# Weight tiles placed 128 bytes further on in SBUF, in a causal convolution with two gated layers

## The chip, the cores and the metric

One core of one Trainium2 chip. The metric is the device time of the whole program in microseconds (us), the median of several runs.

## The reference, cut to what matters

```python
out = np.einsum('hk,bskhg->bshg', softmax(weight), x_unf)   # causal convolution of 7 taps, 8 heads
x = out.reshape(8192, 192)
h = x @ w_in;  x = (h * sigmoid(h)) @ w_out                 # layer 0: 192 -> 2048 -> 192, SiLU
h = x @ w_in2; x = elu(h) @ w_out2                          # layer 1: the same shape, ELU
```

All of it is asked for in float32 precision; the weights are given as float64 and reach the chip as 64-bit words.

## The kernel before, in words

Tokens lie along the free dimension, 512 at a time: 16 blocks `b`. The 192 features are three groups of 64 rows, and the 2048 hidden features are eight chunks `q` of 256. A **unit** is one (layer, block, chunk): 2 x 16 x 8 = 256 units, run one after the other by the loop at the end of the kernel function.

TensorE works in two row halves of 64 partitions, so that two matmuls of 64 rows run side by side. Such a pair is called a **step** here. For precision each operand is split into a rounded part (hi) and a remainder (lo), both of type float32r. A unit has 19 steps:

- `in_products` (L310): 9 steps that make `h` out of the weights `wi` and the tokens `x_hl`.
- `out_products` (L357), two units later: 10 steps that add to the sums `c` and `ab` out of the weights `wo` and the activations `g_hi`, `g_lo`. In order: 2 steps c from g_hi, 2 steps c from g_lo, 4 steps ab from g_hi, 2 steps ab from g_lo.

Each step loads its weights anew (LDWEIGHTS, PEld in the profile), 128 columns per half, except c from g_lo, which loads 66 columns:

```python
C_LO = HP + 2                                   # 66
order = [("c", w_c, 0), ("c", slice(P, P + C_LO), 1), ("ab", w_hi, 0), ("ab", w_lo, 0), ("ab", w_hi, 1)]
```

The weights live in nine places of two tiles each, `wi` and `wo` (pool `wts`), 3072 bytes per partition each. Every slice that a load reads begins a whole number of 128-column blocks, that is of 512 bytes, after the start of its tile. Since 3072 is six times 512, all loads of the program begin at the same offset modulo 512. The weights come from DRAM into `raw` tiles (`load_w`, L88 and L92), are decoded to float32 in `val` with the help of `mag` (`decode_steps`, L110 to L120), and are split into `wi` and `wo` (`split_w`, L127, L128, L141, L143). All but the first two chunks of layer 0 are decoded while matmuls run.

ScalarE and VectorE turn `h` into `g_hi` and `g_lo` (L326 to L338); SyncE issues every DMA.

SBUF is given out pool by pool, in the order in which the pools are opened: `const`, `wts`, `raw`, `mag_p`, `dec`, and then the tiles of tokens and activations. Per partition, the built program before has these start addresses modulo 512: `wi`, `wo`, `raw`, `mag` and `val` 416, the two `x_raw` tiles 416 and 480, `x_hl`, `g_hi`, `g_lo` and the sums on their way out 32.

Of the kernel before, what the change touches and what calls it, by code (L numbers as in the profile page):

```python
# [9 lines left out]
F32 = mybir.dt.float32  # L10
# [12 lines left out]
P = 128  # L23
# [6 lines left out]
W_IN = 3 * P  # L30
W_OUT = 2 * D
RAW = 3

PLACES = NQ + 1
C_LO = HP + 2


@with_exitstack
def kernel(
# [19 lines left out]
    const = ctx.enter_context(tc.tile_pool(name="const", bufs=1))  # L59
    wts = ctx.enter_context(tc.tile_pool(name="wts", bufs=1))  # L60
    raw = ctx.enter_context(tc.tile_pool(name="raw", bufs=RAW))
    mag_p = ctx.enter_context(tc.tile_pool(name="mag_p", bufs=1))
# [19 lines left out]
    IN, OUT, BOTH = slice(0, W_IN), slice(W_IN, W_IN + W_OUT), slice(0, W_IN + W_OUT)  # L82
# [11 lines left out]
    def words(layer, q, cols):  # L94
        w = raw_t[layer, q].bitcast(I32).rearrange("p (n two) -> p n two", two=2)
        return w[:, cols, 0], w[:, cols, 1]

    def decode_steps(layer, q, cols, val=None, mag=None):


        if (layer, q) not in dec_t:
            if mag is None:
                mag = mag_p.tile([P, W_IN + W_OUT], F32, tag="mag", name="mag")
            if val is None:
                val = dec.tile([P, W_IN + W_OUT], I32, tag="val", name="val")
            dec_t[layer, q] = mag, val
        mag, val = (t[:, cols] for t in dec_t[layer, q])
        lower, upper = words(layer, q, cols)
        return [
            lambda: nc.scalar.activation(  # L110
                out=mag, in_=upper.bitcast(F32), func=ACTF.Abs, scale=2.0**-112
            ),
            lambda: nc.vector.tensor_scalar(
                out=val, in0=lower, scalar1=29, scalar2=None, op0=ALU.logical_shift_right
            ),
            lambda: nc.vector.scalar_tensor_tensor(  # L116
                out=val, in0=upper, scalar=-(2**31), in1=val,
                op0=ALU.bitwise_and, op1=ALU.bitwise_or,
            ),
            lambda: nc.vector.scalar_tensor_tensor(  # L120
                out=val, in0=mag.bitcast(I32), scalar=3, in1=val,
                op0=ALU.logical_shift_left, op1=ALU.bitwise_or,
            ),
        ]
# [5 lines left out]
    def split_w(layer, q, cols, eng):  # L130
        if (layer, q) not in wt:
            wt[layer, q] = [
                wts.tile([P, 2, n], F32R, tag=f"{t}{(layer * NQ + q) % PLACES}", name=t)
                for t, n in (("wi", W_IN), ("wo", W_OUT))
# [13 lines left out]
    tap_raw = const.tile([P, 2, TAPS], F32, name="tap_raw")  # L148
    tap_e = const.tile([P, 2, TAPS], F32, name="tap_e")
    tap_w = const.tile([P, 2, TAPS], F32, name="tap_w")  # L150
    tap_m = const.tile([P, 2], F32, name="tap_m")
    tap_s = const.tile([P, 2], F32, name="tap_s")
    tap_r = const.tile([P, 2], F32, name="tap_r")

# [185 lines left out]
    def out_products(u, part=slice(0, None)):  # L340
# [6 lines left out]
        w_hi, w_c, w_lo = (slice(k * P, (k + 1) * P) for k in range(3))  # L347
        order = [("c", w_c, 0), ("c", slice(P, P + C_LO), 1), ("ab", w_hi, 0), ("ab", w_lo, 0), ("ab", w_hi, 1)]
        order = [(*o, i) for o in order for i in range(2)]
# [73 lines left out]
    def next_w(layer, q, *others, val=None):  # L423
        run(decode_steps(layer, q, BOTH, val), *others)
        if q + RAW < NQ:
            load_w(layer, q + RAW)
# [7 lines left out]
    def first_step(q):  # L434
        steps_w[q] = decode_steps(0, q, BOTH)
        return steps_w[q][1]
# [36 lines left out]
    base = where[0, NB - 1, 0]  # L473
    spare = PLACES - NQ
    for q in range(NQ):
# [11 lines left out]
    with tc.manual_schedule():  # L487
# [7 lines left out]
        ab = conv_steps(0, 0, lambda: ps_h.tile([P, 2, TB], F32, tag="h", name="conv")[:, 0, :])  # L495
        c, c_1 = conv_pool_steps(0, 1), conv_pool_steps(1, 1)
        d_in, d_out = (decode_steps(0, 0, cols) for cols in (IN, OUT))
        run(ab, c)
        run(c_1[:4])
# [122 lines left out]
```

## Time and profile before

| what | value |
|---|---|
| median of 3 runs | 1165.93 us (1165.91 to 1166.46) |
| the profiled execution: its own time | 1166.09 us |
| its span, first to last instruction | 1164.3 us |
| granted TensorE clock, mean | 0.997 |
| PE busy | 1140.6 us, 98% of the span |
| PEld busy | 894.1 us, 77% |
| DVE, ACT, POOL busy | 70%, 55%, 5% |

PE is the matmuls, PEld the weight loads, which run beside them. The chain of waits is followed back from the last instruction; 97% of it lies on PE.

### The profile page before, as it was taken

The numbers are of one execution on the slowest core, as the hardware profiler recorded it, in microseconds if no ns is written. First come the engines' busy times: TensorE is split into PE (matmuls) and PEld (weight loads), VectorE is DVE, ScalarE is ACT, GpSimd is POOL, SyncE is SP. The second block draws the span as 40 slices with busy tenths as digits, with TensorE's granted clock in tenths as the row PEclk, the third lists the DMA queues.
The fourth block names the chain that finished last, engine by engine and source line by source line (L and its number), as shares of the span: only waits on it lengthen the run. The fifth ranks groups of instructions, "written<-read, shape, count | busy, mean of one in ns | idle before, by whom it ended". The sixth has DMA issues, their size and how long they took to land.

```text
span 1164.3 us, 22489 instructions
## 1 busy us (share of the span) xinstructions
PE 1140.6 (98%) x9748; PEld 894.1 (77%) x9748; DVE 819.9 (70%) x957; ACT 643.5 (55%) x761; POOL 57.6 (5%) x67
## 2 busy tenths in 40 slices
PE   4899999999999999999999999999999999999998
PEld 3777777777777777777777777777777777777776
DVE  8965546556555555567767787877878777887876
ACT  7655455555545555456775455555455554555554
POOL 7500000000000000000320000000000000000000
PEclk8999999999999999999999999999999999999999
DMA  6310111110111110143201111101111101111100
GB/s 190 103 49 8 35 42 42 42 37 6 42 42 42 42 24 18 42 136 82 83 8 30 33 42 42 42 15 37 33 42 42 42 15 28 42 42 42 29 23 19
DMA packets 31188, 51.11 MB, mean 44 GB/s; under 512 B 3952, under 2 KB 13936, under 8 KB 31088
## 3 DMA queue, kind: packets, MB, share of 16 engines
q1 hardware_dynamic: 31088, 49.67, 16.5%
q8 instruction: 76, 1.25, 0.4%
q14 instruction: 24, 0.20, 0.1%
HBM read 18.98 MB, written 6.29 MB: 22 GB/s over the span
## 4 chain that ended last, share of the span: by engine, by line
PE 97%; DVE 1%; POOL 1%; ACT 0%; SPq 0%; DMA 0%; issue 0%; DVEq 0%; POOLq 0%
PE h L310 46%; PE ab L357 31%; PE c L357 20%; DMA raw<-in_w_dram 0%; POOL conv L289 0%; PE warm L522 0%; DVE g_lo L338 0%; POOL wi L128 0%; SPq L188 0%; DVE x_hl L128 0%; ACT x_hl L127 0%; SPq L88 0%; POOL x_hl L241 0%; DVE val L116 0%; ACT wi L127 0%
## 5 line engine op out<-in xcount | busy, mean ns | idle before, releaser
L310 PE MATMUL h<-x_hl,wi 64*128 64x512 f32 x4608 | 582.9, 394 | 19.5 <-ACT wi L127 13.7
L310 PEld LDWEIGHTS h<-x_hl,wi 64*128 64x128 f32 x4608 | 435.1, 185 | 127.8 <-ACT wi L127 14.6
L357 PE MATMUL ab<-g_hi,wo 64*128 64x512 f32 x2048 | 279.3, 390 | 0.0
L338 DVE TENSOR_TENSOR g_lo<-h,g_hi 128x1024 fp32r<-128x1024 f32 x128 | 156.5, 1223 | 174.3 <-ACT h L327 174.1
L326 ACT ACTIVATE g_hi<-h 128x1024 fp32r<-128x1024 f32 x128 | 131.2, 1025 | 240.1 <-PE h L310 240.1
L331 ACT ACTIVATE g<-h 128x1024 f32<-128x1024 f32 x128 | 131.6, 1028 | 235.5 <-PE h L310 212.0
L357 PEld LDWEIGHTS ab<-g_hi,wo 64*128 64x128 f32 x2048 | 192.5, 184 | 56.5
L333 DVE SCALAR_TENSOR_TENSOR g<-g,h 128x1024 f32<-128x1024 f32 x128 | 156.0, 1219 | 86.4 <-ACT g L332 85.9
L357 PE MATMUL ab<-g_lo,wo 64*128 64x512 f32 x1024 | 162.1, 394 | 0.0
L338 DVE TENSOR_TENSOR g_lo<-g,g_hi 128x1024 fp32r<-128x1024 f32 x128 | 156.9, 1226 | 4.5
L357 PE MATMUL c<-g_lo,wo 64*66 64x512 f32 (+1 forms) x1024 | 160.0, 390 | 0.0
L357 PE MATMUL c<-g_hi,wo 64*128 64x512 f32 x1024 | 160.0, 390 | 0.0
L332 ACT ACTIVATE g<-g 128x1024 f32<-128x1024 f32 x128 | 135.7, 1060 | 3.5
L327 ACT ACTIVATE h<-h 128x1024 f32<-128x1024 f32 x128 | 130.8, 1022 | 0.0
L357 PEld LDWEIGHTS c<-g_hi,wo 64*128 64x128 f32 x1024 | 96.2, 184 | 22.6
L357 PEld LDWEIGHTS ab<-g_lo,wo 64*128 64x128 f32 x1024 | 96.2, 184 | 22.3
L269 DVE SCALAR_TENSOR_TENSOR conv<-x_raw,tap_w,conv 128x512 f32<-128x512 f32 (+1 forms) x180 | 105.8, 626 | 0.5
L357 PEld LDWEIGHTS c<-g_lo,wo 64*66 64x66 f32 (+1 forms) x1024 | 71.5, 136 | 35.6
L336 DVE CAST g_hi<-g 128x1024 fp32r<-128x1024 f32 x128 | 88.9, 694 | 4.5
L379 DVE TENSOR_TENSOR both<-c,both 128x512 f32<-128x512 f32 x32 | 22.1, 692 | 52.0 <-ACT both L378 52.0
L128 POOL TENSOR_TENSOR wi<-val,wi 128x384 fp32r<-128x384 f32 x11 | 11.6, 1056 | 530.6 <-ACT wi L127 530.6
L128 DVE TENSOR_TENSOR x_hl<-conv,x_hl 64x256 fp32r<-64x256 f32 (+1 forms) x47 | 24.0, 534 | 1.2 <-ACT x_hl L127 0.7
(61 smaller groups left out, 325.6 us busy)
## 6 DMA issues: line engine op xcount, KB each, us to landing
x_hl<-x_hl SPq DMA_DIRECT2D x76, 256.0 KB, 3.9
raw<-in_w_dram SPq DMA_DIRECT2D x16, 512.0 KB, 4.4
x_hl<-x_hl SPq DMA_DIRECT2D x34, 128.0 KB, 3.7
x_raw<-in_xT_dram SPq DMA_DIRECT2D x16, 259.0 KB, 3.8
raw<-in_w_dram SPq DMA_DIRECT2D x32, 128.0 KB, 3.1
out_dram<-o SPq DMA_DIRECT2D x16, 256.0 KB, 2.0
x_raw<-in_xT_dram SPq DMA_DIRECT2D x32, 65.5 KB, 3.0
out_dram<-other SPq DMA_DIRECT2D x16, 128.0 KB, 2.3
```

Of the source, the lines that this page charges most:

```text
L128: eng.tensor_sub(out=lo, in0=src, in1=hi.bitcast(F32))
L269: nc.vector.scalar_tensor_tensor(out=y, in0=x, scalar=w, in1=y, op0=ALU.mult, op1=ALU.add)
L310: nc.tensor.matmul(out=h[:, r, :], lhsT=w[ROWS[r], w_lo, ts(of, P)], rhs=x[ROWS[r], 3 * x_lo + part, :], start=n == 0, stop=n == len(order ...
L326: lambda: nc.scalar.activation(out=hi, in_=h, func=ACTF.Silu),
L327: lambda: nc.scalar.activation(out=g, in_=h, func=ACTF.Silu),
L331: lambda: nc.scalar.activation(out=g, in_=h, func=ACTF.Relu, scale=-1.0),
L332: lambda: nc.scalar.activation(out=g, in_=g, func=ACTF.Exp, scale=-1.0),
L333: lambda: nc.vector.scalar_tensor_tensor(out=g, in0=g, scalar=-1.0, in1=h, op0=ALU.add, op1=ALU.max),
L336: lambda: nc.vector.tensor_copy(out=hi, in_=g),
L338: return steps + [lambda: nc.vector.tensor_sub(out=lo, in0=g, in1=hi.bitcast(F32))]
L357: nc.tensor.matmul(out=acc_t[layer, b, f"{name}{r}"][0:m, :], lhsT=wo[ROWS[r], i, cols], rhs=hi_lo[part][ROWS[r], i, :], start=q == 0 and ...
L379: nc.vector.tensor_add(out=to[:, cols], in0=halves[1][:, cols], in1=to[:, cols])
```

## The change

Two tiles that nothing else uses get unused bytes at their end. `tap_m`, in the first pool, becomes 128 bytes longer, so that all that is placed behind it starts 128 bytes later: `tap_s`, `tap_r`, all `wi` and `wo`, all `raw`, and `mag`. `mag` becomes 384 bytes longer, so that all that is placed behind it starts 128 + 384 = 512 bytes later and keeps its offset modulo 512. In the built program `wi`, `wo`, `raw` and `mag` go from 416 to 32 modulo 512; `val`, `x_raw`, `x_hl`, `g_hi`, `g_lo` and the rest stay where they were modulo 512. Every engine has the same instructions, in the same order and with the same waits; line numbers grow by one or two.

```diff
+LINE = 128
...
-                mag = mag_p.tile([P, W_IN + W_OUT], F32, tag="mag", name="mag")
+                mag = mag_p.tile([P, W_IN + W_OUT + 3 * LINE // 4], F32, tag="mag", name="mag")
+                mag = mag[:, BOTH]
...
-    tap_m = const.tile([P, 2], F32, name="tap_m")
+    tap_m = const.tile([P, 2 + LINE // 4], F32, name="tap_m")[:, 0:2]
```

## Rows read from the trace of the kernel before

**Rows 1.** The page, part 1: busy time, share of the span, instructions.
```profile
PE 1140.6 (98%) x9748; PEld 894.1 (77%) x9748; DVE 819.9 (70%) x957; ACT 643.5 (55%) x761; POOL 57.6 (5%) x67
```
**Rows 2.** The page, part 4: the chain that ended last, by engine.
```profile
PE 97%; DVE 1%; POOL 1%; ACT 0%; SPq 0%; DMA 0%; issue 0%; DVEq 0%; POOLq 0%
```
**Rows 3.** The chain in order of time (start us, us, what): steady state, layers 0 and 1.
```profile
63.83 2.10 PE h L310 x18
...
209.67 2.10 PE h L310 x18
211.78 0.93 PE c L357 x8
212.70 1.40 PE ab L357 x12
214.10 2.09 PE h L310 x18
...
218.51 2.10 PE h L310 x18
...
1102.51 2.10 PE h L310 x18
...
1111.35 2.10 PE h L310 x18
...
1142.30 4.18 PE h L310 x36
```
**Rows 4.** Timeline of PE, two units of layer 0 (start us, us, what, count).
```profile
300.48 0.62 PE L357 MATMUL c<-g_lo,wo 64*66 64x512 f32 x4
300.94 1.08 PE L357 MATMUL ab<-g_hi,wo 64*128 64x512 f32 x8
301.86 0.64 PE L357 MATMUL ab<-g_lo,wo 64*128 64x512 f32 x4
302.34 2.25 PE L310 MATMUL h<-x_hl,wi 64*128 64x512 f32 x18
304.43 0.62 PE L357 MATMUL c<-g_hi,wo 64*128 64x512 f32 x4
304.89 0.63 PE L357 MATMUL c<-g_lo,wo 64*66 64x512 f32 x4
305.35 1.10 PE L357 MATMUL ab<-g_hi,wo 64*128 64x512 f32 x8
306.29 0.63 PE L357 MATMUL ab<-g_lo,wo 64*128 64x512 f32 x4
```
**Rows 5.** Groups by line and shape: weight loads (busy us, mean ns | idle before).
```profile
L357 PEld LDWEIGHTS c<-g_hi,wo 64*128 64x128 f32 x1024 | 96.2, 184 | 22.6
L357 PEld LDWEIGHTS c<-g_lo,wo 64*66 64x66 f32 x960 | 65.5, 133 | 32.6
```
**Rows 6.** The chain in order of time, before the first matmul.
```profile
5.53 4.34 DMA raw<-in_w_dram
...
10.29 0.97 DVE val L116
...
21.78 3.78 PE h L310 x16
```
**Rows 7.** Groups by line and shape: the same decode step on tiles at other offsets.
```profile
L116 DVE SCALAR_TENSOR_TENSOR val<-raw,val 128x768 int32<-128x768 int32 x11 | 13.3, 1209 | 0.2
L116 DVE SCALAR_TENSOR_TENSOR val_x<-raw,val_x 128x768 int32<-128x768 int32 x2 | 2.3, 1166 | 0.1
L116 DVE SCALAR_TENSOR_TENSOR val_g<-raw,val_g 128x768 int32<-128x768 int32 x2 | 1.9, 959 | 0.1
```
**Rows 8.** The page, part 2: busy tenths of DVE and granted clock, 40 slices of the span.
```profile
DVE  8965546556555555567767787877878777887876
...
PEclk8999999999999999999999999999999999999999
```
**Rows 9.** The page, part 6: DMA issues (count, KB each, median us to landing).
```profile
x_hl<-x_hl SPq DMA_DIRECT2D x76, 256.0 KB, 3.9
...
x_raw<-in_xT_dram SPq DMA_DIRECT2D x16, 259.0 KB, 3.8
```

## The prediction

> **What bounds the kernel now.** I read the busy shares first: PE is busy for 98% of the span, no other engine for more than 77% [rows 1]. Then the chain of waits, 97% of which is matmuls [rows 2]; so only what changes the pace of the matmuls, or the 21.78 us before the first one [rows 6], can change the time by much. The pace stands in the chain in order of time [rows 3]. From the h block at 209.67 to the next but one at 218.51 two units take 8.84 us, 4.42 us each, or 4.42 / 19 = 0.2326 us a step. In layer 1, from 1102.51 to 1111.35, it is 8.84 us again, and from 63.83 to 1142.30 the program advances 1078.47 / 8.84 = 122.0 such double units: nothing disturbs the pace over 93% of the span. [...]
>
> Inside two units the timeline shows which steps are long and which short [rows 4]. The two steps that load 66 columns take 300.94 - 300.48 = 0.46 us, 0.230 us each. The four behind them take 301.86 - 300.94 = 0.92 us, again 0.230 each, the next two 302.34 - 301.86 = 0.48 us, 0.240 each, and the nine of h 2.09 us, 0.232 each. In the next unit the four behind the short loads take 306.29 - 305.35 = 0.94 us, 0.235 each. So the same kind of step takes 0.230 us in one unit and 0.235 in the next, and the units alternate between 2.10 and 2.09 us for h [rows 3]. The pace has a small swing of its own, some 0.01 us wide, that comes back every two units.
>
> The reader should see three more things. First, a load of 128 columns takes 184 ns and one of 66 columns 133 ns [rows 5], and the steps that run beside the short loads are no shorter than the shortest others, 0.230 us [rows 4]. Against a step of 230 ns a 128-column load ends about 230 - 184 = 46 ns early, a 66-column load about 97 ns early: the loads have slack. Second, nine places of weights and several buffers of x_hl and g take turns, so every address bit from 512 bytes up changes in the trace, and the pattern comes back at 8.84 us regardless. Third, the pattern is the same in layer 0, where VectorE is busy for five to six tenths, and in layer 1, where it is seven to eight tenths [rows 8]: accesses to SBUF by the others, at whatever phase, leave no mark on a step. What the trace can't show is the low part of the address, for all loads begin at 416 modulo 512.
>
> **The change, part by part.**
>
> The weight tiles: 9748 loads [rows 1] begin at 32 instead of 416 modulo 512. No count, no order and no wait changes. A 128-column load reads 512 bytes and crosses one multiple of 512 either way; a 66-column load reads 264 bytes and crosses one from 416 but none from 32. If a crossing costs anything, only the 66-column loads get cheaper, and they have 97 ns to spare; if the new place makes a 128-column load dearer, the first 46 ns of that are hidden. I take **0**. What covers it is the running matmul pair. Without that cover a load that grew by x would cost x - 46 ns per step. The bounds come from the two-step groups of the timeline: every step at the shortest seen, 0.230 us, gives (0.230 - 0.2326) x 19 x 256 = -12.6 us; every step at the longest, 0.240 us, gives +36 us [rows 3, 4]. Zero is nearest to the evidence, since steps with half the load are no quicker.
>
> The raw tiles: their transfers run beside matmuls, except the first ones; there the chain shows one transfer of 4.34 us before decoding starts [rows 6]. The bytes and rows are the same, the destination is 128 bytes further on. No row shows another destination offset for it. The nearest are two kinds of transfer of almost the same size: into x_raw, at 416 and 480 modulo 512, 259 KB land in 3.8 us, and into x_hl, at 32, 256 KB in 3.9 us [rows 9]. They differ in their source too, so their 0.1 us bounds the offset's part either way; I take **0**.
>
> [...]
>
> The decode of the first tiles: raw and mag move, val does not. VectorE's middle step takes 0.97 us on the chain [rows 6]. Later the same step takes 1209 ns with val at 416, 1166 ns with val_x at 416 or 480 and 959 ns with val_g at 32 modulo 512 [rows 7]. The 250 ns between the ends may come from offsets or from what ran beside it; for three such steps at half the size on the path that bounds this term at 0.4 us either way. The nearest row is val_x, 43 ns off, so I take **0**.
>
> All that lies behind mag moves by 512 bytes, which the turning buffers already do without a trace: **0**. tap_s and tap_r are used once, while the chain waits for that first transfer: **0**.
>
> Sum: 1166.09 us (the profiled execution's own time, span 1164.3 plus 1.8 around it) + 0 = 1166.1; that execution lies 0.16 us above the median of the runs, so the forecast for the median is **1165.9 us**, no change.
>
> **The rivals.** About 0.2%, 2.3 us, is what a measurement of this kernel can tell from no change; over 256 x 19 = 4864 steps that is 0.5 ns a step, so the pace need not change by much to count.
>
> Slower, by the swing. The units alternate: behind the 66-column loads the four ab steps take 0.92 us in one unit and 0.94 in the next [rows 4]. The short loads seem to turn the pace over, from a quick phase into a slow one and back. If a load that begins at 32 ends or starts a nanosecond or two differently, the pace may stay in one phase. Its price: with all steps at the slow level of the ab blocks, 1.40 / 6 = 0.2333 us [rows 3], a unit takes 4.433 us instead of 4.42, and 256 x 0.013 = 3.4 us give **1169.3 us**. It decides at the place right behind c from g_lo, from the point where both units show 0.94 us for the four ab steps. For it speaks that so fine a pattern hangs on something as fine; against it, that it has come back unchanged for 122 double units, so it is not easily tipped. The opposite tip, always quick, would win about as little, under the bound of 0.2% or near it, and stays in "no change".
>
> Slower, by a collision. The weights would then begin at 32 modulo 512, just where x_hl and g begin. If the reads of the two got in each other's way at equal offsets, steps would go to the longest seen, 0.240 us: 4.56 us a unit, up to **1201.9 us**. Against it: other engines' reads leave no mark, and the half loads no gain.
>
> Faster, by the end of a collision. The long steps of 0.240 us may be what a weight read and a token read at 416 and 32 cost each other now. If all went to 0.230 us: **1153.3 us**; if half of them, 1159.6. Against it speaks the same as above.
>
> The change may also not do what it says, if the builder rounded the sizes. The addresses of the built program speak against that: they are at 32.
>
> **How the numbers follow.** No change within 0.2%: 0.62. Slower by the swing 0.14, by a collision 0.07, together 0.21 slower. Faster 0.17, most of it for less than the full gain. The range goes down to 1160, which takes in nearly all of the half gain of the faster case, 1159.6, and up to 1171, which takes in the swing (1169.3) with the 0.5 us of bounds at the start and 1.2 us for its price, read from rows in steps of 0.01 us; outside lie the collision and the full gain, under 0.2 together. The forecast's own range is 1163.6 to 1168.2.
>
> **What would show it.** Right: two units at 8.84 us in both layers, loads at 184 and 133 ns, 0.230 us beside the 66-column loads, the first matmul near 21.8 us. The swing case shows h blocks at equal lengths in all units and a double unit near 8.87 us. A collision shows in loads longer than 184 ns and steps of 0.240 us throughout. Wrong I am if the double unit moves by over 0.02 us, for 122 times 0.02 is 2.4 us; then the low bits of the weights' address do count, and my argument from the slack of the loads fails.

## The result, and the profile after

| | before | after |
|---|---|---|
| median | 1166.14 us (6 runs) | 1137.68 us (6 runs, 1137.6 to 1138.2) |
| ratio | | 0.9757, 95% interval 0.9744 to 0.9769 |
| span of the profiled execution | 1164.3 us | 1135.9 us |

The change makes the kernel 28.5 us faster, 2.4%. The forecast was no change, with a range down to 1160 us; it was wrong. (Line numbers after are two higher than before.)

The busy shares of the changed kernel, as in [rows 1]:

```profile
PE 1113.1 (98%) x9748; PEld 894.5 (79%) x9748; DVE 818.7 (72%) x957; ACT 643.1 (57%) x761; POOL 57.4 (5%) x67
```

PE loses 27.5 us of busy time; the other engines keep theirs. The weight loads (PEld) last about as long as before, 184 to 185 ns and 133 ns, as the groups by line and shape show beside [rows 5]:

```profile
L359 PEld LDWEIGHTS c<-g_hi,wo 64*128 64x128 f32 x1024 | 96.6, 185 | 19.9
L359 PEld LDWEIGHTS c<-g_lo,wo 64*66 64x66 f32 x960 | 66.0, 133 | 30.2 <-DVE g_lo L340 0.2
```

The pace is what changed. The chain in order of time (start us, us, what), answering to [rows 3]:

```profile
63.45 0.68 PE h L312 x5
...
201.26 2.04 PE h L312 x18
203.30 0.91 PE c L359 x8
204.21 1.36 PE ab L359 x12
205.56 2.04 PE h L312 x18
...
209.87 2.04 PE h L312 x18
...
214.18 0.90 PE h L312 x7
...
1114.27 4.08 PE h L312 x36
```

Three units take 214.18 - 201.26 = 12.92 us, 4.307 us each instead of 4.42. All blocks now have the same length in every unit: h 2.04 us, c 0.91, ab 1.36; 2.04 / 9, 0.91 / 4 and 1.36 / 6 are all 0.227 to 0.228 us a step. The swing of before is gone. The timeline shows it too: the four ab steps behind the short loads took 0.92 and 0.94 us by turns [rows 4]; in the changed kernel (start us, us, what, count):

```profile
302.64 0.62 PE L359 MATMUL c<-g_lo,wo 64*66 64x512 f32 x4
303.10 1.07 PE L359 MATMUL ab<-g_hi,wo 64*128 64x512 f32 x8
304.00 0.62 PE L359 MATMUL ab<-g_lo,wo 64*128 64x512 f32 x4
304.45 2.20 PE L312 MATMUL h<-x_hl,wi 64*128 64x512 f32 x18
...
306.95 0.62 PE L359 MATMUL c<-g_lo,wo 64*66 64x512 f32 x4
307.40 1.07 PE L359 MATMUL ab<-g_hi,wo 64*128 64x512 f32 x8
308.31 0.62 PE L359 MATMUL ab<-g_lo,wo 64*128 64x512 f32 x4
```

The four take 0.90 and 0.91 us. Between 200 and 500 us the starts of all steps in the trace give a mean of 232.63 ns a step before and 226.67 ns after: 5.96 ns less. Over 4864 steps that would be 29.0 us; the steps that wait for something at the start gain less. Over the 244 steady units [rows 3] it is 244 x 19 x 5.96 ns = 27.6 us. The chain agrees: these units took 1078.47 us before and take 1114.27 - 63.45 = 1050.82 us now, 27.65 us less, of the 28.4 us by which the span is shorter. The rest, just under 0.8 us, lies in the units ahead of these and behind them.

The start tells little. The first matmul of all starts at 12.63 us instead of 12.86. Transfers of 512 KB into raw land in 4.5 us (median) where they took 4.4; the first of them, the one on the chain of before [rows 6], takes 3.80 us instead of 4.34. But in the runs below that first transfer takes 4.1 to 4.7 us with raw at 32 (c128_w32, all66_w32, w32_t160), as in the changed kernel, and 4.5 to 4.8 us with raw at 416 (w416_t416, c128_w416, all66_w416), as before. The ranges overlap, and at equal offsets it differs by 0.31 us or more (4.34 us before, 4.65 in c128_w416), so the 0.54 us can't be put down to raw's offset.

### The profile page after: what moved, and what is told of

Same layout as the page of the kernel before. It is cut to its first block, busy times and chain, and to the rows that moved or that the text cites. A ratio compares the mean times of both kernels' runs of the same rounds, so it can differ in the third digit from the quotient of the medians.

```text
span 1135.9 us, 22489 instructions
## 1 busy us (share of the span) xinstructions
PE 1113.1 (98%) x9748; PEld 894.5 (79%) x9748; DVE 818.7 (72%) x957; ACT 643.1 (57%) x761; POOL 57.4 (5%) x67
## 4 chain that ended last, share of the span: by engine, by line
PE 95%; DVE 3%; issue 1%; DMA 0%; ACT 0%; POOL 0%; DVEq 0%; SPq 0%
PE h L312 45%; PE ab L359 30%; PE c L359 20%; DVE val L118 1%; DVE conv L271 1%; DVE g_lo L340 1%; DVE val L115 1%; DVE x_hl L130 0%; DMA x_raw<-in_xT_dram 0%; DVE val L122 0%; DVE conv L269 0%; POOL wi L130 0%; ACT x_hl L129 0%; DVE x_hl L232 0%; DVE wi L130 0%
## 5 line engine op out<-in xcount | busy, mean ns | idle before, releaser
L312 PE MATMUL h<-x_hl,wi 64*128 64x512 f32 x4608 | 570.2, 389 | 18.6 <-ACT wi L129 12.6
L312 PEld LDWEIGHTS h<-x_hl,wi 64*128 64x128 f32 x4608 | 434.6, 185 | 112.2 <-ACT wi L129 12.6
L359 PE MATMUL ab<-g_hi,wo 64*128 64x512 f32 x2048 | 273.9, 386 | 0.0
L359 PE MATMUL ab<-g_lo,wo 64*128 64x512 f32 x1024 | 157.9, 386 | 0.0
```

Source lines behind the costliest of these rows:

```text
L312: nc.tensor.matmul(out=h[:, r, :], lhsT=w[ROWS[r], w_lo, ts(of, P)], rhs=x[ROWS[r], 3 * x_lo + part, :], start=n == 0, stop=n == len(order ...
L359: nc.tensor.matmul(out=acc_t[layer, b, f"{name}{r}"][0:m, :], lhsT=wo[ROWS[r], i, cols], rhs=hi_lo[part][ROWS[r], i, :], start=q == 0 and ...
```

## The experiments

Each kernel ran once, beside a run of the kernel before, which took 1166.3 to 1166.6 us. "Distance" is the weights' offset minus that of the token tile, x_hl or g, modulo 512: 384 before, 0 in the changed kernel. The edits are against the kernel before; only the lines that take the place of old ones are shown. In `n // 4`, n is the number of bytes added per partition: behind `2 +` it moves the weights and all that follows, behind `W_OUT +` it moves all that is placed behind `mag` further still.

### Whose offset counts?

**w416_t416**: the tokens come to the weights.

```diff
+mag = mag_p.tile([P, W_IN + W_OUT + 384 // 4], F32, tag="mag", name="mag")[:, BOTH]
```

> Weights stay at 416 modulo 512, all tokens and activations move from 32 to 416. Theory D (what counts is the distance between the weights' offset and the offset of the token tile that streams meanwhile): distance 0 as in the changed kernel, so every step 0.2267 us and about 1137.7 us. Theory W (what counts is the weights' own offset): 416 as before, so 0.2326 us a step and about 1166 us.

Measured: 1138.26 us.

**w32_t160**: both move, the distance stays at 384.

```diff
+tap_m = const.tile([P, 2 + 128 // 4], F32, name="tap_m")[:, 0:2]
```

> Weights at 32 as in the changed kernel, but the tokens and activations move to 160, so that the weights lie 128 bytes behind them, as before. Theory D: the pace of before, 0.2326 us a step, about 1166 us. Theory W: the pace of the changed kernel, 0.2267 us, about 1137.7 us.

Measured: 1166.43 us.

**w160_t32**: the distance is 128 with the other sign.

```diff
+tap_m = const.tile([P, 2 + 256 // 4], F32, name="tap_m")[:, 0:2]
...
+mag = mag_p.tile([P, W_IN + W_OUT + 256 // 4], F32, tag="mag", name="mag")[:, BOTH]
```

> Weights at 160, tokens at 32: the weights 128 bytes ahead of the tokens instead of behind. Theory D in the form that only equal offsets are free of collisions: slow, about 1166 us. Theory D in the form that only weights behind the tokens collide: about 1137.7 us. Theory W says nothing of 160 by itself.

Measured: 1166.04 us.

**w0_t0**: both at a multiple of 512.

```diff
+tap_m = const.tile([P, 2 + 96 // 4], F32, name="tap_m")[:, 0:2]
...
+mag = mag_p.tile([P, W_IN + W_OUT + 384 // 4], F32, tag="mag", name="mag")[:, BOTH]
```

> Weights and tokens both at 0. Theory D: distance 0, 0.2267 us a step, about 1137.7 us. [...] Theory W has no value for 0.

Measured: 1137.62 us.

The chain in order of time of w416_t416 shows the blocks of the changed kernel:

```profile
206.15 2.04 PE h L310 x18
208.19 0.91 PE c L357 x8
209.10 1.36 PE ab L357 x12
```

and that of w32_t160 those of before:

```profile
205.60 2.09 PE h L310 x18
207.69 0.93 PE c L357 x8
208.61 1.40 PE ab L357 x12
210.01 2.10 PE h L310 x18
```

Weights at 416 are fast if the tokens are at 416, and weights at 32 are slow if the tokens are at 160. So the distance decides, not the weights' own place: theory D, in the form that only equal offsets are free, holds in all four (1138.26 and 1137.62 us at equal offsets, 1166.43 and 1166.04 at others); W falls in the first two, and D's other form, in which only weights behind the tokens collide, falls in w160_t32. That a load crosses a multiple of 512 or not plays no part either: in w416_t416 the 66-column loads cross one, and it takes 1138.26 us. With everything on multiples of 128 bytes, in w0_t0, a step takes 226.67 ns, as in the changed kernel.

### What distances are free?

**w288_t32**, **w96_t32**, **w64_t32**, **w224_t32**, **w256_t32**, **w128_t32**, **w192_t32** keep the tokens at 32 and move the weights alone, in steps of 32 bytes. The first, for example:

```diff
+tap_m = const.tile([P, 2 + 384 // 4], F32, name="tap_m")[:, 0:2]
...
+mag = mag_p.tile([P, W_IN + W_OUT + 128 // 4], F32, tag="mag", name="mag")[:, BOTH]
```

The two numbers ahead of `// 4` are 384 and 128 here, then 192 and 320, 160 and 352, 320 and 192, 352 and 160, 224 and 288, 288 and 224.

> Distance 256 modulo 512. Theory E (only equal offsets modulo 512 are free of collisions, and any other distance costs the same): 0.2326 us a step, about 1166 us. Theory H (the pattern repeats every 256 bytes): 0.2267 us, about 1137.7 us.

> Distance 64, half of what was tried so far. Theory E: about 1166 us. Theory G (the cost grows with the distance): between, near 1152 us if it is proportional up to 128. Theory N (both starts within one block of 128 bytes are as good as equal): about 1137.7 us.

> Distance 32, the smallest that the allocation of tiles gives. Theory E: about 1166 us. Theory G: near 1145 us, a quarter of the cost. Theory N: about 1137.7 us.

> Distance 192, that is 64 bytes behind modulo 256. Theory P (the step depends on the distance modulo 256, and only 0 is free): slow, 1166 to 1170 us. Theory S (the sign counts: ahead by 64 was 1168.8, behind by 64 may be free): 1138 us or less.

> Distance 224, 32 bytes behind modulo 256. Theory P: slow, 1166 to 1170 us. Theory S: 1138 us or less.

> Distance 96. Theory P (only 0 modulo 256 is free): between its neighbours 64 and 128, 1166 to 1169 us. If some distance lets the steps fall under 0.2267 us, it must be here or at 160.

> Distance 160. Theory P: between its neighbours 128 (1166.0) and 192 (1155.6), about 1161 us, if the cost changes steadily from step to step.

| distance modulo 256 | kernels | us | mean step, ns |
|---|---|---|---|
| 0 | changed, w416_t416, w0_t0, w288_t32 | 1137.6 to 1138.3 | 226.67 |
| 32 | w64_t32 | 1169.55 | 233.28 |
| 64 | w96_t32 | 1168.82 | 233.03 |
| 96 | w128_t32 | 1174.67 | 234.38 |
| 128 | before, w32_t160, w160_t32 | 1165.9 to 1166.6 | 232.63 |
| 160 | w192_t32 | 1172.00 | 233.90 |
| 192 | w224_t32 | 1155.62 | 230.45 |
| 224 | w256_t32 | 1167.86 | 233.03 |

(The mean step is that of all starts between 200 and 500 us.) Distance 256 is as good as 0 (w288_t32, 1138.19 us), and 384, before, costs the same as 128 (w160_t32, 1166.04 us). So the pattern repeats after 256 bytes, 64 columns: theory H, not E. These two pairs show it; the other distances were tried on one side of 256 only. Of the distances tried only 0 lets every step fall to 226.67 ns, as theory P has it. The loss at the others is neither steady (G falls) nor a matter of a shared block of 128 bytes (N falls), and its size was guessed wrongly three times: 1155.62 us at 192 instead of 1166 to 1170, 1174.67 at 96 instead of 1166 to 1169, 1172.00 at 160 instead of 1161. Of the sign, S, only this much is left, that 192 costs 13.2 us less than 64; 160 and 224 cost 2.7 and 1.7 us less than 96 and 32, little beyond the 0.2% that the prediction took for the limit of a measurement, or under it. The worst, at 96, is slower than the kernel before; its chain in order of time:

```profile
206.67 2.10 PE h L310 x18
208.78 0.94 PE c L357 x8
209.72 1.40 PE ab L357 x12
211.12 2.11 PE h L310 x18
```

Distances between multiples of 32 were not tried.

### Is it the tile that streams?

**x416_g32** gives x_hl alone the weights' offset; every place that makes an x_hl tile is changed as in the last two lines.

```diff
+    def x_hl_tile():
+        t = xs.tile([P, 6 * TB + 128], F32R, tag="x_hl", name="x_hl")
+        return t[:, 96 : 96 + 6 * TB].rearrange("p (n t) -> p n t", t=TB)
...
-        t = x_hl[0, 0] = xs.tile([P, 6, TB], F32R, tag="x_hl", name="x_hl")
+        t = x_hl[0, 0] = x_hl_tile()
```

> Weights at 416 as before, g_hi and g_lo at 32 as before, x_hl alone moved to 416. Theory D (the distance between the weights that load and the tokens that stream at that moment): the 9 steps of h in each unit at 0.2267 us, the 10 of c and ab as before: 1166.1 - 256 x 9 x 0.0059 = 1152.5 us, and in the trace h blocks of 2.04 us beside ab blocks of 1.40. If some tile other than the one that streams counts: 1166 or 1138 us.

Measured: 1160.41 us, faster by 6.1 us than the run of before beside it, where 13.6 were expected: the direction of theory D, under half its size. Its timeline of PE:

```profile
300.98 2.25 PE L314 MATMUL h<-x_hl,wi 64*128 64x512 f32 x18
303.07 0.63 PE L361 MATMUL c<-g_hi,wo 64*128 64x512 f32 x4
...
305.39 2.23 PE L314 MATMUL h<-x_hl,wi 64*128 64x512 f32 x18
307.46 0.62 PE L361 MATMUL c<-g_hi,wo 64*128 64x512 f32 x4
```

The h blocks take 303.07 - 300.98 = 2.09 and 307.46 - 305.39 = 2.07 us, not 2.04. Between 200 and 500 us the steps of h take 230.55 ns on average where they took 233.0 before, and the ten others 232.3 ns as before: what x_hl's offset changes is the steps that stream x_hl, but not down to the floor. The single steps, as differences of starts in the trace in ns, tell more. Line 1: the changed kernel behind a wait, from 32.14 us, 18 steps. Lines 2 and 3: the nine steps of h of two neighbouring units of x416_g32, from 292.19 and from 287.81 us.

```
306 229 234 236 224 231 235 229 232 231 227 226 227 227 226 227 227 226
234 231 234 235 225 230 236 229 233
230 236 229 232 231 227 226 227 227
```

Even at distance 0 the steps come down to 226 and 227 ns only after a run-in, ten steps in line 1 (five and three behind the next two waits, from 36.96 and 41.77 us). Line 2 goes through almost the same run-in, and its block ends where the floor would begin; line 3 gets there after five steps. A step's length thus depends on the steps before it, too. What is carried from one step to the next, no row shows.

The same stretches answer another question, whether the two halves of a step get in each other's way. In the steady units the halves start 3 to 4 ns apart. Behind these waits they start 16 to 64 ns apart from the second step on, and the steps keep their lengths: 226 and 227 ns in the changed kernel from 39.10 us on, with 53 to 57 ns between the halves, and 229 to 238 ns in the kernel before from 37.48 us on, with 30 to 41 ns. So the loss doesn't hang on how the two halves lie to each other.

### What part do the short loads and the length of the loads have?

**c128_w416** and **c128_w32** load 128 columns for c from g_lo as for all others, with the tiles of before and of the change.

```diff
-C_LO = HP + 2
+C_LO = P
```

> The tiles of the kernel before, but c from g_lo loads 128 columns like all others. Theory K (the short loads turn the pace over between a quick and a slow phase, as the prediction's second case had it): one phase alone in all units, 4.416 or 4.435 us a unit, so 1165 or 1170 us. Theory D says only that it stays slow, for the distance is 384.

Measured: 1165.28 us, steps of 232.38 ns on average: theory K's quick phase, worth 1.2 us against the run of before beside it, within the 0.2% that the prediction took for the limit of a measurement. In the trace its steps repeat about 228, 230, 232, 241, 232, 231 and 232 ns in all units, the sequence that before only every other stretch between the short loads had.

> The changed kernel, but c from g_lo loads 128 columns. Theory D: the distance is 0, so no step notices its load: 0.2267 us everywhere, about 1137.7 us, as with 66 columns. Theory B (the gain needs the 66-column loads, which cross no multiple of 512 from 32): well above 1138 us, up to the 1165 us of the same loads at 416.

Measured: 1137.67 us. The gain does not need the 66-column loads; theory B falls.

**all66_w416** and **all66_w32** load 66 columns nearly everywhere, with the tiles of before and of the change. They leave out the products beyond column 66, so their matmuls also write 66 rows of a sum instead of 128; no run separates this from the shorter load.

```diff
+            m = C_LO if n % 8 else P
             nc.tensor.matmul(
-                out=h[:, r, :], lhsT=w[ROWS[r], w_lo, ts(of, P)],
+                out=h[0:m, r, :], lhsT=w[ROWS[r], w_lo, of * P : of * P + m],
...
-            m = cols.stop - cols.start
+            m = P if last or q == 0 and n in (0, 4) else C_LO
+            cols = slice(cols.start, cols.start + m)
```

> The tiles of the kernel before; all loads but the first of each sum and two of the nine of h take 66 columns instead of 128, so most products are left out beyond column 66. Theory C (what the steps lose at a distance of 384 is time in which a load and a token stream read at once, so half as long a load loses about half): the 0.0059 us above 0.2267 falls to about 0.003, about 1152 us. Theory F (the loss does not depend on how long the load is): about 1166 us.

Measured: 1155.44 us. The steps fall from 232.63 to 230.32 ns, that is by 2.3 of the 5.96 ns: nearer to theory C than to F, though not quite half. Some loads keep 128 columns; the mean over a unit goes from 121.5 to 72.5 columns, to 60%, and the loss above 226.67 ns from 5.96 to 3.65 ns, to 61%. It is no fixed proportion, though, for in c128_w416 the mean goes up to 128 columns and the loss down to 5.71 ns. Its groups by line and shape show the short loads:

```profile
L311 PEld LDWEIGHTS h<-x_hl,wi 64*66 64x66 f32 x3584 | 245.1, 133 | 162.7 <-POOL wi L128 2.8 <-ACT x_hl L227 0.8 <-issue 0.8
```

> The changed kernel with nearly all loads cut to 66 columns; products beyond column 66 are left out. Theory D: the steps are at a floor that has nothing to do with the loads, 0.2267 us, about 1137.7 us. [...]

Measured: 1138.06 us, steps of 226.67 ns, as with full loads; its chain in order of time:

```profile
205.93 2.04 PE h L311 x18
207.97 0.91 PE c L359 x8
208.88 1.36 PE ab L359 x12
```

At distance 0 nearly all loads at 66 columns leave the steps at 226.67 ns; at distance 384 they bring them from 232.63 to 230.32 ns, unless there the narrower sums count. That the change removes time in which weight loads and the token streams beside them delay each other is the author's reading of these numbers; that it is the loads' length, and how a delay would arise, is argued and not shown. Why a step at distance 0 takes 226.67 ns stays open.

## Why the prediction was wrong, point by point

**What bounds the kernel** was right: the pace of the matmuls, 4.42 us a unit, in both layers, and 97% of the gain is in it. That address bits from 512 up leave the pace alone was right too (two units take 8.84 us throughout); by w288_t32, 1138.19 us, the bit worth 256 does so as well.

**The failed step** is the first term of the sum, "The weight tiles ... I take **0** ... Zero is nearest to the evidence, since steps with half the load are no quicker." It measured -27.65 us over the steady units, beyond its fast bound of -12.6. Two readings led to it. The first took the slack of a load, 46 ns before the next pair, for proof that its place can't matter. But between 200 and 500 us a 128-column load takes 184.4 ns on average before (184 to 188) and 184.0 ns after, only 0.4 ns less, while the time from one pair's start to the next falls by 5.96 ns: a load that ends in time can still go with a longer step. The second took the two steps at 66 columns for a test of half a load. It looked one step too late: between 200 and 500 us a load starts 2 to 4 ns after the start of the pair before its own (in the timeline of before, the loads of c from g_lo at 300.25 us and their own pair at 300.48), so the steps beside the short loads are the second of c from g_hi and the first of c from g_lo, which take 229 to 235 ns, 232.3 on average between 200 and 500 us, against 232.63 for all. These are no shorter to speak of either, but two short loads in a row lie among seventeen long ones, and a step depends on those before it; when nearly all loads are short, all66_w416 shows the steps 2.3 ns quicker. The third argument, that accesses by other engines leave no mark, fits the steady pace (8.84 us for two units in both layers, with VectorE busy for five to eight tenths) and was beside the point: what moved the time in these runs, from 1166 to 1138 us, is the distance between TensorE's own two operands.

**The bounds** of that term were too narrow on the fast side. The floor was put at the shortest group of before, 0.230 us, which gave -12.6 us. In the kernel before no step between 200 and 500 us is shorter than 0.228 us; in the changed kernel they take 0.2267 us.

**The rival "faster, by the end of a collision"** came nearest. It put the loss on weights at 416 beside tokens at 32, and the steps fall from 232.63 to 226.67 ns when either goes to the other's offset (the changed kernel, w416_t416); that it is their reads that cost each other time was its assumption, which no run shows. It had a chance of 0.17, most of that for less than its full price; and that price, 1153.3 us, lies 15.6 us above what was measured, because it rests on the same floor of 0.230 us. **"Slower, by a collision"** made the same assumption with the sign turned round: at equal offsets the steps are the shortest, 226.67 ns, not the longest. **"Slower, by the swing"** was right in that the short loads turn the pace over between two phases (c128_w416 shows one phase alone, 232.38 ns a step), but it did not come about: in the changed kernel all steps between 200 and 500 us take 226 or 227 ns.

The **terms at the start**, put at 0 within 0.5 us, can't be told apart from the 0.8 us outside the steady units. (The 21.78 us that the prediction took for the first matmul is only where the chain meets the matmuls; the first one starts at 12.86 us.)

## What to carry to other kernels

Where weight loads run beside streaming matmuls and the steps come in several lengths, compare the start addresses of the tiles that load as weights and of the tiles that stream: here equal offsets modulo 256 bytes were worth 2.4%, for some padding. Only 64-row float32r pairs of 512 columns with a load beside each were tried. An edit that changes the size of an early tile can shift that distance, as 128 bytes more in `tap_m` did here (from 384 to 0), so a gain or loss behind such an edit should be checked against the addresses. Slack of a load against the next matmul does not show that the load is free: here loads that ended some 46 ns early went with steps 5.96 ns longer.

## What was not expected of the hardware

In these runs the step's length depends on the distance between two addresses modulo 256 bytes, with losses from 3.8 ns (192) to 7.7 ns (96) in no steady order. At distance 0 the steady steps take 226.67 ns on average for 512 columns, with loads of 66 and of 128 columns alike. And behind a wait, or where a stretch at distance 0 begins, the steps seen needed a run-in of three to ten before they reached it.
